# Scores of the second token group by three fp32r products, and its probabilities normalised behind the product with the values

## The chip, the cores and the metric

The kernel runs on one core of one Trainium2 chip. The metric is the time of one execution on the device in microseconds (us), given as the median of the runs shown. TensorE (PE in the profile) multiplies matrices, VectorE (DVE) and ScalarE (ACT) work element by element, GpSimd (POOL) hardly takes part, and SyncE (SP) issues most DMAs. Each engine works through its own instructions in the order in which the program gives them.

## The reference, cut to what matters

```python
# attention: batch 2, 12 heads, 448 tokens, head size 64, causal
scores = (q @ k.T) / sqrt(64);  scores[j > i] = -1e9
p = exp(scores - max(scores));  p = p / (sum(p) + 1e-9)
x = (p @ v) reshaped to 896 tokens x 768
# first layer: 768 -> 2048 -> 768
h = x @ w_in;  g = h if h >= 1, 0 if h <= -1, (h + 1)**2 / 4 between
y = g @ w_out
# second layer: 768 -> 1536 -> 768
out = (silu(y @ w_gate) * (y @ w_val)) @ w_out2
```

All inputs and the output are fp32. q and k are scaled up by about 22, so that the scores are large and need nearly full fp32 precision.

## The kernel before

The time has two parts. In the first, the attention is worked out and, from its middle on, the first products of the first layer are slipped in between. In the second, only the large products of the two layers run.

The attention works by units. A unit is one batch and one pair of heads for one of two token groups: group 0 is the first 224 tokens of each sequence, group 1 the last 224. There are 12 units of group 0, of one step each, and then 12 units of group 1, of two steps each: step kind 2 has 112 tokens against 336 keys, kind 3 has 112 tokens against all 448. The two heads of a pair lie in partitions 0 to 63 and 64 to 127 of one tile `qk_t`. A step goes through these functions:

- `scores`: PE multiplies q and k of each head in plain fp32 into the PSUM tile `s`, and adds the causal mask as one more product (`mask_b` times an identity, bf16).
- `greatest`: DVE takes the row maxima (`tensor_reduce`, L427) and scales them (`mx`, L429).
- `exps`: ACT takes the exponentials into `p` and their row sums into `sm` (L441).
- `normalize`: DVE turns the sums into reciprocals (L452, L453) and multiplies `p` by them (L465).
- `turn` and `turned`: PE transposes `p` into the PSUM tile `t`, and ACT copies it to `pt` (L485).
- `values`, once a unit: PE multiplies `pt` and the values into the PSUM tile `o`.
- `x_hi`, `x_lo`: ACT rounds `o` to fp32r (`xh`, L518) and DVE takes the rest (`xl`, L522).

The layers multiply split operands: each fp32 matrix is the sum of two fp32r parts, hi and lo, and `mm3` issues three fp32r products, hi hi, hi lo and lo hi. The weights come in a narrowing form and are made into such parts in four operations (L102, L105, L108 and the pair L213 on ACT and L214 on DVE, called a tick each here). `Weights.tick` issues the next of these, and `TICKS` and `LATER` say how many at each step of the two groups.

The loop of the attention runs over steps k. At each k it goes through the list `ORDER[kind]`, and each word in it issues one function, for step k+1, k, k-1 or k-2. `fill` issues in group 0 a few products of zeros (`zeros`, L532), and from step 14 on a third of the 18 products of one 128-column block of the first layer for group 0 (`h_products`, tile `mm`, one PSUM bank). When a block is complete, ACT and DVE work out its activation (`h_relu` L341, `h_max` L346 and L347, `g_hi` L352, `g_lo` L356), and only L347 frees the bank for the next block. `follow` keeps an issued group of products together on PE; the rest of the order on each engine is set by a list scheduler at build time from the order of issue and its priorities, which is why the order is shown below beside the diff.

Of the kernel before, what the change touches and what calls it, by code (L numbers as in the profile page):

```python
# [8 lines left out]
F32 = mybir.dt.float32  # L9
F32R = mybir.dt.float32r  # L10
# [20 lines left out]
HOLD = (12, 6, 4, 2)  # L31
AHEAD = 3
LASTB = 2
WBUFS = 4
# [4 lines left out]
LOW_V = 999  # L39
NORM_P = 0  # L40
TURN0 = "A"
TURN1 = "A"
NORM0 = "V"
NORM1 = "V"
SEVEN = (1, 2, 3, 4, 5, 6, 7, 8, 9, 10)
# [8 lines left out]
S_LOW = "V"  # L54
PINNED = 2

ORDER = {
    0: "copy scores max fill values x_hi weights norm x_lo turn exp relu square g_hi g_lo".split(),
    2: "copy scores fill max relu values exp norm x_hi x_lo turn square g_hi g_lo weights".split(),
    3: "copy scores fill max relu values exp norm x_hi x_lo turn square g_hi g_lo weights".split(),  # L60
}
TICKS = (1, 0, 1)
LATER = (1, 0, 3)


@with_exitstack
def fused_kernel(ctx: ExitStack, tc: tile.TileContext, qk, v, w_in, w_out, w_gv, w_o2, out):
# [3 lines left out]
    edge = ctx.enter_context(tc.tile_pool(name="edge", bufs=1, side="right"))  # L71
    half_b = edge.tile([128, 56], F32, name="half_b")[:, :1]
    half_x = const.tile([128, 32], F32, name="half_x")[:, :1]
    xy = ctx.enter_context(tc.tile_pool(name="xy", bufs=2))
# [246 lines left out]
    def bank():  # L321
        pool = banks.pop(0)
        banks.append(pool)
        return pool.tile([128, 512], F32, tag="mm", name="mm")

    def h_products(g, f, free=((True, True), (True, True))):

        xh, xl = xT[g]
        wh, wl = W.get(f)
        ps = bank()  # L330
        for c in range(KC):
            sl = slice(c * 128, (c + 1) * 128)
            mm3(ps[:, :N], wh[:, sl], wl[:, sl], xh[:, c], xl[:, c], c == 0, c == KC - 1, free[c % 2])
            if c % 2 and c < KC - 1:
                yield
        yield ps

    def h_relu(f, ps):

        r = ev.tile([128, N], F32, tag="r", name="r")  # L340
        nc.scalar.activation(out=r, in_=ps[:, :N], func=AF.Relu, bias=half_b, scale=0.5)  # L341
        return f, ps, r

    def h_max(f, ps, r):
        q = ev.tile([128, N], F32, tag="t", name="q")
        nc.vector.scalar_tensor_tensor(out=q, in0=r, scalar=1.0, in1=r, op0=ALU.min, op1=ALU.mult)  # L346
        nc.vector.tensor_tensor(out=q, in0=ps[:, :N], in1=q, op=ALU.max)  # L347
        return 0, f, q, gt0
# [22 lines left out]
    with ExitStack() as ph:  # L371
# [7 lines left out]
        mask_b = lp.tile([128, C], BF16, name="mask_b")  # L379
        ld, st, pts = {}, {}, {}  # L380

        def load(u):
            if u >= len(units):
                return
            g, n = units[u]
            src = n[0] * NP + n[1]
            qk_t = lp.tile([128, 672], F32, tag="qk", name="qk_t", bufs=AHEAD + 1)
            v_t = lp.tile([C, 4, 128], F32, tag="v", name="v_t", bufs=AHEAD + 4)
# [6 lines left out]
            ld[u] = qk_t, v_t  # L395

        def scores(k):
# [6 lines left out]
            for i, (off, w, q0) in enumerate(reversed(SEGS[j])):  # L404
                for h in range(2):
                    hd = slice(h * D, (h + 1) * D)
                    follow(
                        nc.tensor.matmul, i == h == 0,
                        out=s[:C, h, off:off + w], lhsT=qk_t[hd, q0:q0 + C], rhs=qk_t[hd, k0:k0 + w],
                        start=(i == 0), stop=False, skip_group_check=True,  # L410
                    )
            for off, w, _ in SEGS[j]:
                for h in range(2):
                    follow(
                        nc.tensor.matmul, False,
                        out=s[:C, h, off + w - C:off + w], lhsT=ident_b[:C, :], rhs=mask_b[:C, :],
                        start=False, stop=True, skip_group_check=True,
                    )
            st[k] = {"s": s}

        def greatest(k):

            _, j = steps[k]
            s, segs = st[k]["s"], SEGS[j]
            mx = s[:C, 0, 504:508].rearrange("p (i h) -> p i h", h=2)
            for i, (off, w, _) in enumerate(segs):
                nc.vector.tensor_reduce(out=mx[:, i], in_=s[:C, :, off:off + w], axis=AX.X, op=ALU.max)  # L427
            m = pp.tile([C, 2, 2], F32, tag="mx", name="mx")
            nc.vector.tensor_scalar(  # L429
                out=m[:, :len(segs)], in0=mx[:, :len(segs)], scalar1=-0.125, scalar2=None, op0=ALU.mult)  # L430
            st[k]["mx"] = m

        def exps(k):

            _, j = steps[k]
            s, mx = st[k]["s"], st[k]["mx"]
            sm = pp.tile([C, 2, 2], F32, tag="sm", name="sm")
            p = pp.tile([C, 2, S], F32, tag="p", name="p")
            for i, (off, w, _) in enumerate(SEGS[j]):
                for h in range(2):  # L440
                    nc.scalar.activation(  # L441
                        out=p[:, h, off:off + w], in_=s[:C, h, off:off + w], func=AF.Exp,
                        bias=mx[:, i, h:h + 1], scale=0.125, accum_out=sm[:, i, h:h + 1],
                    )
            st[k].update(p=p, sm=sm)

        def normalize(k):
            _, j = steps[k]
            p, segs = st[k]["p"], SEGS[j]
            sm = st[k].pop("sm")  # L450
            m = sm[:, :len(segs)]
            nc.vector.tensor_scalar(out=m, in0=m, scalar1=1e-9, scalar2=None, op0=ALU.add)  # L452
            nc.vector.reciprocal(out=m, in_=m)  # L453
            for i, (off, w, _) in enumerate(segs):
                if j == 0 and NORM_P:
                    nc.gpsimd.tensor_tensor(
                        out=p[:, :, off:off + w], in0=p[:, :, off:off + w],
                        in1=sm[:, i].unsqueeze(2).to_broadcast([C, 2, w]), op=ALU.mult,
                    )
                else:  # L460
                    norms = NORM0 if j == 0 else NORM1
                    for h in range(2):
                        ph, r = p[:, h, off:off + w], sm[:, i, h:h + 1]
                        if norms[(2 * k + h) % len(norms)] == "V":
                            nc.vector.tensor_scalar(out=ph, in0=ph, scalar1=r, scalar2=None, op0=ALU.mult)  # L465
                        else:
                            nc.scalar.mul(out=ph, in_=ph, mul=r)

# [19 lines left out]
        def values(k):  # L488
# [25 lines left out]
            g, (b, hp) = units[u]  # L514
            return [o[:, :GT]] + [t[:, hp, b * GT:(b + 1) * GT] for t in xT[g]]

        def x_hi(o, xh, xl):
            nc.scalar.copy(out=xh, in_=o)  # L518
            return o, xh, xl

        def x_lo(o, xh, xl):
            nc.vector.tensor_tensor(out=xl, in0=o, in1=xh.bitcast(F32), op=ALU.subtract)  # L522

# [6 lines left out]
        def zeros(n):  # L530
# [4 lines left out]
        make_identity(nc, ident)  # L535
        nc.vector.memset(mask_b, 0.0)
        nc.vector.memset(half_b, 0.5)

        nc.scalar.activation(out=half_x, in_=half_b, func=AF.Exp)
        nc.gpsimd.affine_select(  # L540
            out=mask_b[:C, :], in_=mask_b[:C, :], compare_op=ALU.is_ge, fill=MASK,
            base=0, pattern=[[-1, C]], channel_multiplier=1,
        )
# [18 lines left out]
        first1 = next(k for k, (u, j) in enumerate(steps) if j == 2)  # L562
        fresh_o, half_o, half, whole, split_h = [], [], [], [], []
        for k in range(-1, last + 2):
# [3 lines left out]
            for op in ORDER[kind]:  # L568
# [4 lines left out]
                elif op == "max" and lead:  # L573
                    greatest(k + 1)
                elif op == "exp" and lead:
                    exps(k + 1)
# [5 lines left out]
                elif op == "values" and pv:  # L582
                    assert not fresh_o and not half_o and "t" not in st[k - 2]
                    fresh_o.append(values(k - 2))
                elif op == "x_hi" and fresh_o:
                    half_o.append(x_hi(*fresh_o.pop()))
                elif op == "x_lo" and half_o:
# [20 lines left out]
        while done < EARLY or fresh or half or whole or split_h:  # L608
# [8 lines left out]
            if done < EARLY:  # L617
                filler()
                W.tick()
        assert not fresh_o and not half_o  # L620

# [288 lines left out]
```

## Time and profile before

| what | us |
|---|---|
| runs | 585.08, 597.69, 585.05 |
| median | 585.08 |
| profiled execution, its own time | 585.47 |
| its span, first to last instruction | 583.7 |
| attention with the first products in it | about 0 to 146 |
| products of the layers alone | about 146 to 583.7 |

[...] PE is busy 575.5 us, DVE 489.8 us and ACT 271.1 us. Busy times overlap a little: an instruction's time begins before the one ahead of it has ended, so that the distance from start to start is the better measure of what one costs.

### The profile page before, as it was taken

The page shows a single profiled execution, that of the slowest core. Times are in us where ns is not written, and L with a number is a line of the kernel's source. Part 1 is how long each engine was busy: PE and PEld are TensorE (multiplying, and loading weights), DVE is VectorE, ACT ScalarE, POOL GpSimd, SP SyncE. Part 2 cuts the span into 40 slices and gives each one's busy share as a digit, 9 for nine tenths or more (in the row PEclk, how much of TensorE's full clock was granted, in tenths as well). Part 3 has the DMA queues.
Part 4 walks back from the last instruction along what each step waited for, and adds up shares of the span by engine and source line. Part 5 has one row for each costly group of instructions (what it writes and reads, how often), then busy time and mean ns, then how long its engine had stood idle before and what let it go on. Part 6 is the DMA issues. An engine that isn't in the chain of part 4 may idle for free.

```text
span 583.7 us, 8503 instructions
## 1 busy us (share of the span) xinstructions
PE 575.5 (99%) x3167; PEld 498.8 (85%) x3172; DVE 489.8 (84%) x899; ACT 271.1 (46%) x544; POOL 0.9 (0%) x7
## 2 busy tenths in 40 slices
PE   9999999998999999999999999999999999999997
PEld 5766766667999999999999999999999999999996
DVE  2999999973896988787778899999898398999990
ACT  3887777664533444111211165554454244346441
POOL 0000000000000000000000000000000000000000
PEclk9999999999999999999999999999999999999999
DMA  8566554300131233787788711363532133730011
GB/s 259 173 182 210 174 188 144 136 2 2 55 118 45 90 109 120 230 269 207 238 292 244 271 68 56 108 190 108 176 107 98 55 115 109 277 127 16 17 62 65
DMA packets 26009, 80.38 MB, mean 138 GB/s; under 512 B 2928, under 2 KB 10672, under 8 KB 25968
## 3 DMA queue, kind: packets, MB, share of 16 engines
q1 hardware_dynamic: 21792, 73.54, 39.1%
q10 hardware_dynamic: 4176, 6.29, 2.9%
q8 instruction: 25, 0.41, 0.3%
q14 instruction: 16, 0.13, 0.1%
HBM read 70.78 MB, written 9.04 MB: 137 GB/s over the span
## 4 chain that ended last, share of the span: by engine, by line
PE 83%; DVE 13%; ACT 2%; DMA 1%; issue 0%; ACTq 0%
PE mm L84 35%; PE mm L719 27%; PE mm L849 13%; DVE s L427 3%; DVE p L465 2%; PE mm L86 2%; PE s L84 1%; DVE wt L108 1%; PE mm L532 1%; DVE wt L105 1%; ACT p L441 1%; DVE wl L214 1%; DMA wraw<-w_in 1%; PE s L86 1%; PE t L86 1%; DVE wt L102 1%
## 5 line engine op out<-in xcount | busy, mean ns | idle before, releaser
L213 ACT CAST wh<-wt 128x768 fp32r<-128x768 f32 (+1 forms) x43 | 34.7, 807 | 94.2 <-PE mm L84 46.9
L84 PE MATMUL mm<-gl,wh 128*128 128x448 f32 x192 | 70.1, 365 | 0.0
L84 PE MATMUL mm<-gh,wh 128*128 128x448 f32 x192 | 70.1, 365 | 0.0
L84 PE MATMUL mm<-gh,wl 128*128 128x448 f32 x192 | 70.1, 365 | 0.0
L84 PE MATMUL mm<-xh,wh 128*128 128x448 f32 x165 | 62.5, 379 | 2.3 <-DVE q L347 2.3
L441 ACT ACTIVATE p<-s,mx 112x112 f32<-112x112 f32 (+3 forms) x96 | 46.3, 496 | 20.6 <-DVE mx L429 15.1
L84 PE MATMUL mm<-xh,wl 128*128 128x448 f32 x138 | 50.4, 365 | 0.0
L84 PE MATMUL mm<-xl,wh 128*128 128x448 f32 x138 | 50.4, 365 | 0.0
L214 DVE TENSOR_TENSOR wl<-wt,wh 128x768 fp32r<-128x768 f32 (+1 forms) x43 | 39.4, 916 | 10.0 <-ACT wh L213 9.6
L105 DVE SCALAR_TENSOR_TENSOR wt<-wraw,wt 128x768 int32<-128x768 int32 (+1 forms) x51 | 47.1, 923 | 0.8
L108 DVE SCALAR_TENSOR_TENSOR wt<-wraw,wt 128x768 int32<-128x768 int32 (+1 forms) x51 | 47.0, 922 | 0.5
L849 PE MATMUL mm<-ul,oh 128*128 128x448 f32 x126 | 46.0, 365 | 0.0
L849 PE MATMUL mm<-uh,oh 128*128 128x448 f32 x126 | 46.0, 365 | 0.0
L849 PE MATMUL mm<-uh,ol 128*128 128x448 f32 x126 | 46.0, 365 | 0.0
L427 DVE TENSOR_REDUCE s<-s 112x2 f32<-112x224 f32 (+3 forms) x48 | 35.4, 744 | 7.5 <-PE s L86 7.4
L719 PE MATMUL mm<-yh,wh 128*128 128x448 f32 x108 | 39.4, 365 | 0.0
L719 PE MATMUL mm<-yh,wl 128*128 128x448 f32 x108 | 39.4, 365 | 0.0
L719 PE MATMUL mm<-yl,wh 128*128 128x448 f32 x108 | 39.4, 365 | 0.0
L84 PEld LDWEIGHTS mm<-gl,wh 128*128 128x128 f32 x192 | 36.1, 188 | 2.9
L84 PEld LDWEIGHTS mm<-gh,wl 128*128 128x128 f32 x192 | 36.1, 188 | 2.9
L84 PEld LDWEIGHTS mm<-gh,wh 128*128 128x128 f32 x192 | 36.1, 188 | 2.8
L84 PEld LDWEIGHTS mm<-xh,wh 128*128 128x128 f32 x165 | 31.0, 188 | 5.6 <-DVE q L347 3.4
(140 smaller groups left out, 1366.4 us busy)
## 6 DMA issues: line engine op xcount, KB each, us to landing
wraw<-w_in SPq DMA_DIRECT2D x16, 768.0 KB, 4.5
wraw<-w_gv SPq DMA_DIRECT2D x14, 768.0 KB, 4.4
wraw<-w_out SPq DMA_DIRECT2D x12, 768.0 KB, 4.9
araw<-w_gv SPq DMA_DIRECT2D x20, 384.0 KB, 4.6
wraw<-w_o SPq DMA_DIRECT2D x9, 768.0 KB, 4.3
n<-at ACTq DMA_DIRECT2D x26, 192.0 KB, 4.5
qk_t<-qk SPq DMA_DIRECT2D x12, 336.0 KB, 3.3
wraw<-n SPq DMA_DIRECT2D x5, 768.0 KB, 4.3
```

Of the source, the lines that this page charges most:

```text
L84: return product(*args, **kw)
L86: return tc.keep_in_program_order(product(*args, **kw))
L102: yield nc.vector.tensor_scalar(out=t, in0=w[:, :, 1], scalar1=3, scalar2=0x3FFFFFF8, op0=ALU.logical_shift_left, op1=ALU.bitwise_and,)
L105: yield nc.vector.scalar_tensor_tensor(out=t, in0=w[:, :, 1], scalar=-0x40000000, in1=t, op0=ALU.bitwise_and, op1=ALU.bitwise_or,)
L108: yield nc.vector.scalar_tensor_tensor(out=t, in0=w[:, :, 0], scalar=29, in1=t, op0=ALU.logical_shift_right, op1=ALU.bitwise_or,)
L213: nc.scalar.copy(out=wh[:, :n], in_=t)
L214: (nc.vector if i < LOW_V else nc.gpsimd).tensor_tensor(out=wl[:, :n], in0=t, in1=wh[:, :n].bitcast(F32), op=ALU.subtract,)
L427: nc.vector.tensor_reduce(out=mx[:, i], in_=s[:C, :, off:off + w], axis=AX.X, op=ALU.max)
L441: nc.scalar.activation(out=p[:, h, off:off + w], in_=s[:C, h, off:off + w], func=AF.Exp, bias=mx[:, i, h:h + 1], scale=0.125, accum_out=sm ...
L465: nc.vector.tensor_scalar(out=ph, in0=ph, scalar1=r, scalar2=None, op0=ALU.mult)
L719: nc.tensor.matmul(out=ps[:, :N], lhsT=w[a][:, sl], rhs=rows[c][b], start=(first and c == i == 0), stop=(last and c == i == 2), skip_group ...
L849: nc.tensor.matmul(out=ps, lhsT=w[a][:, sl], rhs=rows[c][b], start=(not more and c == e == 0), stop=(c == 5 and e == 2), skip_group_check= ...
```

## The change

For group 1 the parts hi and lo of `qk_t` are made once a unit (`apart_qk`: ACT copies to `qh`, DVE subtracts to `ql`), and the scores are three fp32r products of them for each head, in place of one fp32 product. In steps of kind 2 the mask is no longer a product: DVE's `tensor_tensor_reduce` adds a mask tile, scales by -0.125, writes `s` back and takes the minimum, for each head, which is the bias that the exponential wants; the reduction and L429 fall away there. Steps of kind 3 keep the mask product and the reduction. `normalize` no longer multiplies `p` in group 1. The sums of a unit's two steps lie in one tile, whose reciprocals are taken once a unit; four small fp32 products with a broadcast operand bring them into the layout of `o`, in the same bank; ACT copies them out (`rb`), and DVE multiplies `o` by them (`x_norm`). The parts `xh` and `xl` are then made from `rb`.

The lists in `ORDER` are written anew, with the words `x` and `apart`; `TICKS` gives one tick in three steps in group 0 in place of two, `LATER` four in three steps as before but spread differently; `PINNED` goes from 2 to 9. Ahead of two blocks of the first layer in group 1 stands a product of 1 x 8 (`strip`). The branches under `HM` don't run.

```diff
-PINNED = 2
+PINNED = 9
+STRIPS = (1, 2)
+TTR = (2,)
+HM = 0
...
-    2: "copy scores fill max relu values exp norm x_hi x_lo turn square g_hi g_lo weights".split(),
+    2: "copy turn scores fill max values relu x norm x_hi square x_lo exp g_hi g_lo apart weights".split(),
...
-TICKS = (1, 0, 1)
-LATER = (1, 0, 3)
+TICKS = (0, 0, 1)
+LATER = (1, 1, 2)
...
+        def apart_qk(u):
...
+            hi = lp.tile([128, 672], F32R, tag="qh", name="qh", bufs=QB)
+            lo = lp.tile([128, 672], F32R, tag="ql", name="ql", bufs=QB)
+            split(raw, hi, lo)
...
+            if j:
+                (off, w, q0), = SEGS[j]
+                hi, lo = halves[u]
+                for i, (a, b) in enumerate(((hi, hi), (hi, lo), (lo, hi))):
+                    for h in range(2):
+                        hd = slice(h * D, (h + 1) * D)
+                        follow(
+                            nc.tensor.matmul, i == h == 0,
+                            out=s[:C, h, off:off + w], lhsT=a[hd, q0:q0 + C], rhs=b[hd, k0:k0 + w],
...
-            for off, w, _ in SEGS[j]:
+            for off, w, _ in () if j in TTR else SEGS[j]:
...
+            if j in TTR:
+                off, w, _ = segs[0]
+                for h in range(2):
+                    part = s[:C, h, off:off + w]
+                    nc.vector.tensor_tensor_reduce(
+                        out=part, in0=part, in1=mask[:, S - w:], scale=-0.125, scalar=3.0e38,
+                        op0=ALU.add, op1=ALU.min, accum_out=m[:, 0, h:h + 1],
+                    )
...
+            if j == 2:
+                return
+            sm = sms[u]
+            nc.vector.tensor_scalar(out=sm, in0=sm, scalar1=1e-9, scalar2=None, op0=ALU.add)
+            nc.vector.reciprocal(out=sm, in_=sm)
+            if j == 0:
...
+            for i in range(2 if j else 0):
+                for h in range(2):
+                    follow(
+                        nc.tensor.matmul, False, out=o[h * D:(h + 1) * D, 256 + i * C:256 + (i + 1) * C],
+                        lhsT=sm[:, i, h:h + 1].to_broadcast([C, D]), rhs=ident[:C, :C],
...
+            if j:
+                r = pp.tile([128, GT], F32, tag="rb", name="rb", bufs=2)
+                nc.scalar.copy(out=r, in_=o[:, 256:256 + GT])
...
+        def x_norm(o, r, xh, xl):
+            if r is None:
+                return o, xh, xl
+            nc.vector.tensor_tensor(out=r, in0=o, in1=r, op=ALU.mult)
+            return r, xh, xl
```

On PE, in the middle of group 1, the scores of a step of kind 2 and what follows them stood like this before (`s` scores, `mm` products slipped in, `o` values, `t` transposes; L84 and L86 are lines of the helpers):

```order
L84 MATMUL s<-qk_t 112x336
L86 MATMUL s<-qk_t 112x336
L86 LDWEIGHTS ident_b
L86 MATMUL s<-mask_b,ident_b 112x112
...
L84 MATMUL mm<-xh,wh 128x448
...
L84 MATMUL o<-pt,v_t 64x224
L86 MATMUL o<-pt,v_t 64x224 x5
L86 MATMUL o<-pt,v_t 64x112 x2
L84 MATMUL t<-ident,p 112x112
```

And so they stand in the change, where L89 and L91 are the same lines of the helpers:

```order
L89 MATMUL s<-qh 112x336
L91 MATMUL s<-qh 112x336
L91 MATMUL s<-ql,qh 112x336 x2
L91 MATMUL s<-qh,ql 112x336 x2
L89 MATMUL o<-pt,v_t 64x224
L91 MATMUL o<-pt,v_t 64x224 x5
L91 MATMUL o<-pt,v_t 64x112 x2
L91 MATMUL o<-ident,sm 64x112 x4
L89 MATMUL mm<-xh,wh 128x448
```

Six score products stand for two, the mask products are gone, four products of the sums follow the values, and here, where a new block begins, the products slipped in come behind the values and no longer ahead of them.

On DVE, in the middle of group 1, one stretch of a unit before (`s` reduction, `p` normalising, `q` and `gl` activation of a block, `wt` a tick):

```order
L465 TENSOR_SCALAR p<-p,sm 112x336 x2
L346 SCALAR_TENSOR_TENSOR q<-r 128x448
L427 TENSOR_REDUCE s<-s 112x2
L347 TENSOR_TENSOR q<-mm,q 128x448
L429 TENSOR_SCALAR mx<-s 112x2
L452 TENSOR_SCALAR sm<-sm 112x2
L522 TENSOR_TENSOR xl<-o,xh 128x224
L453 RECIPROCAL sm<-sm 112x2
L105 SCALAR_TENSOR_TENSOR wt<-wraw,wt 128x768
```

The same place in the change, where the two rows named ISA are the masked reduction and the row that writes out its result:

```order
L577 TENSOR_TENSOR rb<-o,rb 128x224
L374 TENSOR_TENSOR gl_3_1414<-q,gh_3_1413 128x448
L478 TENSOR_REDUCE s<-s 112x2
L585 TENSOR_TENSOR xl<-rb,xh 128x224
L479 TENSOR_SCALAR mx<-s 112x2
L101 TENSOR_TENSOR ql<-qk_t,qh 128x672
L471 ISA s,mx<-s,mask 112x336
L471 ISA mx 112x1
L504 TENSOR_SCALAR sm<-sm 112x4
```

The normalising of `p` is gone, and `rb`, `ql` and the masked reduction have come in.

On PE near the end of the attention, where the seventh block (`mm_1627` before) ends and the eighth (`mm_1748`) begins:

```order
L86 MATMUL mm_1627<-xl_75,wh_1435 128x448
L86 MATMUL mm_1627<-xh_74,wl_1436 128x448
L84 MATMUL t_1731<-ident_102,p_1638 112x112
L86 MATMUL t_1731<-ident_102,p_1638 112x112 x3
...
L84 MATMUL mm_1748<-xh_74,wh_1566 128x448
```

In the change these blocks are `mm_1739` and `mm_1865`:

```order
L91 MATMUL mm_1739<-xh_75,wl_1619 128x448
L89 MATMUL t_1858<-ident_103,p_1806 112x112
L91 MATMUL t_1858<-ident_103,p_1806 112x112 x2
...
L89 MATMUL o_1872<-pt_1813,v_t_1420 64x224
L91 MATMUL o_1872<-pt_1813,v_t_1420 64x224 x5
...
L91 MATMUL o_1872<-ident_103,sm_1705 64x112 x4
L89 MATMUL t_1899<-ident_103,p_1847 112x112
L91 MATMUL t_1899<-ident_103,p_1847 112x112 x3
...
L89 MATMUL mm_1865<-xh_75,wh_1759 128x448
```

Between the two blocks there was one group of transposes, and now there are two and the values of a unit.

## Rows read from the trace of the kernel before

**Rows 1.** The page's first part: busy us, share of span, instructions.

```profile
PE 575.5 (99%) x3167; PEld 498.8 (85%) x3172; DVE 489.8 (84%) x899; ACT 271.1 (46%) x544; POOL 0.9 (0%) x7
```

**Rows 2.** Windows by stage: length, busy us of each engine, clock, DMA share.

```profile
15.00:45.00 30.00, 29.55 (x272) 20.40 (x272) 29.64 (x109) 26.83 (x104) 0.00 (x0) 1.00 0.63 186
45.00:80.00 35.00, 34.78 (x250) 23.48 (x246) 35.00 (x91) 25.86 (x64) 0.00 (x0) 1.00 0.57 186
...
110.00:146.00 36.00, 33.84 (x234) 25.13 (x231) 22.26 (x58) 19.54 (x48) 0.00 (x0) 1.00 0.09 34
146.00:347.00 201.00, 201.00 (x993) 186.25 (x993) 165.47 (x276) 61.02 (x98) 0.00 (x0) 1.00 0.53 171
```

**Rows 3.** The chain that ended last: start, length, what.

```profile
146.17 200.64 PE mm L84 x990
```

**Rows 4.** Timeline of PE over one unit of group 1: start, length, instruction.

```profile
113.30 0.63 PE L84 MATMUL s<-qk_t 64*112 64x448 f32 x1
113.31 0.63 PE L86 MATMUL s<-qk_t 64*112 64x448 f32 x1
113.77 0.54 PE L84 MATMUL s<-qk_t 64*112 64x448 f32 x1
...
114.24 0.31 PE L86 MATMUL s<-mask_b,ident_b 112*112 112x112 bf16 x2
114.37 0.45 PE L84 MATMUL mm<-xh,wh 128*128 128x448 f32 x1
114.65 0.36 PE L86 MATMUL mm<-xl,wh 128*128 128x448 f32 x1
...
115.67 0.26 PE L84 MATMUL t<-ident,p 112*112 112x112 f32 x1
...
116.53 0.53 PE L84 MATMUL s<-qk_t 64*112 64x336 f32 x1
...
117.28 0.31 PE L86 MATMUL s<-mask_b,ident_b 112*112 112x112 bf16 x2
117.41 0.45 PE L84 MATMUL mm<-xh,wh 128*128 128x448 f32 x1
...
118.84 0.40 PE L84 MATMUL o<-pt,v_t 112*64 112x224 f32 x1
...
120.32 0.31 PE L84 MATMUL t<-ident,p 112*112 112x112 f32 x1
...
121.04 0.63 PE L84 MATMUL s<-qk_t 64*112 64x448 f32 x1
```

**Rows 5.** Windows of nine middle units, the last of them and their sum.

```profile
121.04:128.72 7.68, 7.68 (x55) 5.32 (x55) 4.91 (x15) 4.36 (x12) 0.00 (x0) 1.00 0.00 0
sum 71.49, PE 70.31 PEld 48.25 DVE 66.88 ACT 49.49 POOL 0.00; mean PE 7.81 PEld 5.36 DVE 7.43 ACT 5.50 POOL 0.00
```

**Rows 6.** The chain between 90 and 112 us, all on DVE.

```profile
93.59 0.61 DVE p L465 x2
...
94.67 0.77 DVE s L427
...
97.03 0.73 DVE p L465 x2
97.76 0.53 DVE q L347
98.29 0.30 DVE xl L522
...
101.13 0.85 DVE wl L214
```

**Rows 7.** Groups on ACT from 57 to 129 us: count, busy us, mean ns.

```profile
L213 ACT CAST wh<-wt 128x768 fp32r<-128x768 f32 x6 | 5.0, 836 | 5.9 <-DVE wt L108 5.9
...
L518 ACT CAST xh<-o 128x224 fp32r<-128x224 f32 x10 | 3.5, 346 | 0.7 <-PE o L86 0.6
```

**Rows 8.** Timeline of PE near the end of the attention, with its wait.

```profile
131.57 0.45 PE L86 MATMUL t<-ident,p 112*112 112x112 f32 x3
133.30 0.47 PE L84 MATMUL mm<-xh,wh 128*128 128x448 f32 x1 [1.27 <-DVE q L347]
```

More of the change, by code (lines that the diff above doesn't have):

```diff
@@ L32 @@
 AHEAD = 3
+QB = 2
+VB = AHEAD + 4
+PB = 3
+QKB = AHEAD + 1
 LASTB = 2
@@ L39 @@
 LOW_V = 999
-NORM_P = 0
 TURN0 = "A"
 TURN1 = "A"
-NORM0 = "V"
-NORM1 = "V"
 SEVEN = (1, 2, 3, 4, 5, 6, 7, 8, 9, 10)
@@ L54 @@
 S_LOW = "V"
-PINNED = 2
+PINNED = 9
+STRIPS = (1, 2)
+TTR = (2,)
+HM = 0
 ORDER = {
-    0: "copy scores max fill values x_hi weights norm x_lo turn exp relu square g_hi g_lo".split(),
-    2: "copy scores fill max relu values exp norm x_hi x_lo turn square g_hi g_lo weights".split(),
-    3: "copy scores fill max relu values exp norm x_hi x_lo turn square g_hi g_lo weights".split(),
-}
-TICKS = (1, 0, 1)
-LATER = (1, 0, 3)
+    0: "copy scores fill values x x_hi apart weights x_lo max turn exp g_hi relu norm square g_lo".split(),
+    2: "copy turn scores fill max values relu x norm x_hi square x_lo exp g_hi g_lo apart weights".split(),
+    3: "norm copy turn scores fill max values x relu exp apart x_hi square g_hi g_lo weights x_lo".split(),
+}
+TICKS = (0, 0, 1)
+LATER = (1, 1, 2)
 @with_exitstack
@@ L324, in bank, with strip @@
         return pool.tile([128, 512], F32, tag="mm", name="mm")
+    def strip(ps, w, x):
+        nc.tensor.matmul(
+            out=ps[:1, 448:456], lhsT=w[:, :1], rhs=x[:, :8], start=True, stop=True, skip_group_check=True)
     def h_products(g, f, free=((True, True), (True, True))):
@@ L330, in h_products @@
         ps = bank()
+        if g and f in STRIPS:
+            strip(ps, wh, xh[:, 0])
         for c in range(KC):
@@ L395, in load @@
             ld[u] = qk_t, v_t
+        halves = {}
+        def apart_qk(u):
+            if not (0 <= u < len(units) and units[u][0]):
+                return
+            raw = ld[u][0]
+            hi = lp.tile([128, 672], F32R, tag="qh", name="qh", bufs=QB)
+            lo = lp.tile([128, 672], F32R, tag="ql", name="ql", bufs=QB)
+            split(raw, hi, lo)
+            halves[u] = hi, lo
         def scores(k):
@@ L402, in scores @@
             k0 = GT if j == 0 else 0
-            for i, (off, w, q0) in enumerate(reversed(SEGS[j])):
+            if j:
[7 more added lines that the diff above has]
+                            out=s[:C, h, off:off + w], lhsT=a[hd, q0:q0 + C], rhs=b[hd, k0:k0 + w],
+                            start=(i == 0), stop=i == 2 and j in TTR, skip_group_check=True,
+                        )
+            for i, (off, w, q0) in enumerate(() if j else reversed(SEGS[j])):
                 for h in range(2):
@@ L514, in values, with x_hi, x_lo @@
             g, (b, hp) = units[u]
[L515 to L522, printed above, removed]
+            sm = sms.pop(u)
+            for i in range(2 if j else 0):
[3 more added lines that the diff above has]
+                        lhsT=sm[:, i, h:h + 1].to_broadcast([C, D]), rhs=ident[:C, :C],
+                        start=True, stop=True, skip_group_check=True,
+                    )
+            if j:
+                r = pp.tile([128, GT], F32, tag="rb", name="rb", bufs=2)
+                nc.scalar.copy(out=r, in_=o[:, 256:256 + GT])
+            else:
+                r = None
+            return [o[:, :GT], r] + [t[:, hp, b * GT:(b + 1) * GT] for t in xT[g]]
+        def x_norm(o, r, xh, xl):
[3 more added lines that the diff above has]
+            return r, xh, xl
+        def x_hi(x, xh, xl):
+            nc.scalar.copy(out=xh, in_=x)
+            return x, xh, xl
+        def x_lo(x, xh, xl):
+            nc.vector.tensor_tensor(out=xl, in0=x, in1=xh.bitcast(F32), op=ALU.subtract)
         for u in range(AHEAD):
@@ L541, in fused_kernel @@
             out=mask_b[:C, :], in_=mask_b[:C, :], compare_op=ALU.is_ge, fill=MASK,
+            base=0, pattern=[[-1, C]], channel_multiplier=1,
+        )
+        nc.gpsimd.affine_select(
+            out=mask[:, S - C:], in_=mask[:, S - C:], compare_op=ALU.is_ge, fill=MASK,
             base=0, pattern=[[-1, C]], channel_multiplier=1,
@@ L562, in fused_kernel @@
         first1 = next(k for k, (u, j) in enumerate(steps) if j == 2)
-        fresh_o, half_o, half, whole, split_h = [], [], [], [], []
+        fresh_o, whole_o, half_o, half, whole, split_h = [], [], [], [], [], []
         for k in range(-1, last + 2):
@@ L574, in fused_kernel @@
                     greatest(k + 1)
+                elif op == "apart" and lead and steps[k + 1][1] != 2:
+                    apart_qk(steps[k + 1][0] + 1)
                 elif op == "exp" and lead:
@@ L619, in fused_kernel @@
                 W.tick()
-        assert not fresh_o and not half_o
+        assert not fresh_o and not whole_o and not half_o
     gt1 = gctx.enter_context(tc.tile_pool(name="gt1", bufs=1))
```

79 lines of the change are left out of this document (41 added, 38 removed).

## The prediction

> **What bounds the kernel now.** I read the page's busy times first: PE 99% of the span, DVE 84%, ACT 46% [rows 1]. A share over the whole span says little, so next come the windows by stage. From 146 us on PE is busy without a gap, and the chain that ended last runs there through nothing but products, 200.64 us for 990 of them, 0.203 us each [rows 2, 3]. The change touches none of these, so the 437.5 us from there to the end stay. Everything is decided between 0 and 146 us.
>
> There DVE looks like the bound: 29.64 of 30 us in group 0, 35.00 of 35 us from 45 to 80, and the chain runs through DVE's instructions one after the other [rows 2, 6]. But PE reads 34.78 of 35 in the same window. To see which of the two sets the pace I followed PE's timeline through one unit of group 1, start to start [rows 4]: scores of the 448 step 0.94 (113.30 to 114.24), their mask 0.13, six products slipped in 1.30, eight transposes 0.86, scores of the 336 step 0.75, mask 0.13, six products 1.43, values 1.48, six transposes 0.72. That is 7.74, and nothing in it is a gap except about 0.1 in the 1.43. The shortest unit lasts 7.68 us, and the nine middle units together 71.49 [rows 5], so PE stood still for 71.49 - 9 x 7.68 = 2.4 us in all of them. PE is the bound of group 1, with DVE close behind (66.88 busy in 71.49), until DVE runs out of ticks at about 111 us and idles (22.26 of the last 36) [rows 2, 5]. A lighter DVE is worth only the gaps of PE; a lighter PE counts twelvefold.
>
> **PE, part by part.** A plain fp32 product runs as two instructions: 0.47 from 113.30 to 113.77, and as long again to the mask. The two heads start 0.01 us apart, so they run side by side, in different rows of the array [rows 4]. An fp32r product of 448 columns costs 1.30 / 6 = 0.217 with its share of the edges. 0.94 is 4.3 times that, so I read a fp32 product as four such passes, 0.87, and 0.07 of edge. For 336 columns the same gives 0.163 a pass and 0.10 of edge in the 0.75. Three passes and the same edge: 3 x 0.217 + 0.07 = 0.72, and 3 x 0.163 + 0.10 = 0.59. With the mask of the 336 step gone (0.13) a unit saves 0.22 + 0.16 + 0.13 = 0.51. If no edge were left, 0.68; if each product paid a whole edge, 0.51 - 2 x 0.07 - 2 x 0.10 = 0.17.
>
> The four products that spread the sums are new. The values, fp32 too and in the same layout, take 1.48 for 784 columns of each head [rows 4]; 224 more columns are 0.42. At the price of transposes, 0.12 for one of 112 columns, eight instructions not side by side would be 0.96. I take 0.42, since they have the shape of the values and stand right behind them. Per unit PE then changes by -0.51 + 0.42 = -0.09, twelve units -1.1 us. The bounds are -0.68 + 0.42 = -0.26 (-3.1 us) and -0.17 + 0.96 = +0.79 (+9.5 us). So the three products save about what the sums cost.
>
> [...]
>
> **DVE and ACT.** Per unit DVE loses the normalising of `p`, 0.61 + 0.73, one reduction, 0.77, and three small rows of about 0.07 [rows 6]: 2.32. It gains two masked reductions of 336 columns; the nearest row reads PSUM and SBUF as they do, 0.53 for 448 columns, and `xl` 0.30 for 224, hence 0.42 each, and 0.07 to write each result, 0.97. The split adds 0.85 x 672 / 768 = 0.74, and `x_norm` a copy of `xl`, 0.30. Net -2.32 + 2.01 = -0.31 a unit, -3.7 us in all. Four ticks move out of group 0 (4 x about 0.85) into the end of group 1, where DVE idled. ACT gains a copy of 672 columns (0.836 x 672 / 768 = 0.73) and one of 224 (0.35) [rows 7], +1.08 on a mean of 5.50 in a unit of 7.68 [rows 5]: covered while nothing waits for ACT at once. Queued behind the copy to `qh` are the exponentials and the copy to `pt`. For the latter PE's order helps: between the eight transposes and the values that need their copy there now stand the 448 scores, six products, six transposes and the 336 scores, some 3.5 us, where 0.88 and 1.3 stood before.
>
> **Gaps of PE.** Of the 2.4 us in the middle units I take 2.0 back, as DVE no longer runs full. Near the end PE waits 1.27 us for L347 to free the bank [rows 8]; by the new order 0.72 + 1.48 + 0.42 + 0.86 of other work lies there, so 1.2 goes. In group 0 PE has 0.45 us without work in 30 [rows 2], and its zero products stay as many; fewer ticks give back at most that, 0.4. Against it I set 1.0 for new waits on ACT, which gets 20% more work (bounds 0 and 3; a tenth of a unit's 1.08 each time), and 0.2 for the two 1 x 8 products.
>
> **Sum.** 585.47 is the profiled execution's own time, 583.7 of it span. -1.1 - 2.0 - 1.2 - 0.4 + 1.0 + 0.2 = -3.5, so 582.0; it lies 0.4 above the median of the runs, which makes **581.6 us**. About 2%, 11.7 us, is what a measurement of this kernel can tell from no change; the forecast lies within it.
>
> **Rivals.**
> - *Every product pays its weight load.* Scores save 0.17 a unit, not 0.51: 12 x 0.34 = +4.1, 585.7 us. For it: 0.47 and 0.47 can be read so. [...] Chance 0.15. [...]
> - *The masked reduction runs at half rate.* 24 x 0.42 = +10 us on DVE, +6.4 with its savings. That is 6.4 / 12 = 0.53 a unit; DVE then sets the pace (7.43 + 0.53 = 7.96 against 7.68, 12 x 0.28 = 3.4), and nothing else is won: 585.1 + 3.4 = 588.5 us. For it: no row shows this instruction. Against: its two inputs are read at full rate in `q`. [...] Chance 0.07.
> - *The heads don't run side by side in the new products.* Scores cost 6 x 0.217 + 0.07 = 1.37 and 6 x 0.163 + 0.10 = 1.08, a unit +0.43 + 0.20, and the sums 0.84: +1.47, against -0.09 in the forecast 1.56 x 12 = 18.7 us more, 600 us. This is the slower side. It decides from about 1.2 us a unit on. For it: an fp32r product in half the rows stands nowhere in the trace. Against: the fp32 ones with the same rows do pair. Chance 0.05.
> - *PE gets all of it.* No edges (-3.1), all gaps (2.4 + 1.3 + 0.4), no waits on ACT: 585.1 - 7.2 + 0.2 = 578.1, and 575.6 if the sums' products hide half of their 0.42. Chance 0.15.
>
> **How the numbers follow.** The forecast's own cluster, 578.5 to 585, has 0.58. The range, 575.5 to 588.6, takes in the fast rival, the paid loads and the half rate, and leaves out the unpaired heads and what I don't foresee. Faster by over 2% (below 573.4) needs more than all gaps and all edges, 0.05; slower by over 2% (above 596.8) is the unpaired heads, 0.05; within 2% 0.90.
>
> **What will show it.** Scores on PE in the changed profile: 0.72 and 0.59 from their start to the next group, or 0.80 and more each if loads are paid, or 1.1 to 1.4 if unpaired. The sums' products: 0.42 between values and next group. Masked reductions on DVE 0.42 apart, or 0.8. A unit about 7.6 us, and the products alone starting at about 142.6 rather than 146.2. The prediction is wrong if PE waits for `pt` or `p` in each unit (ACT), or if the stage after 146 us changes.

## The result, and the profile after

The changed kernel takes 590.5 us (591.06, 590.13, 590.80, 590.20). Against the kernel before the ratio is 1.0094, interval 1.0069 to 1.0118: under 1% slower, and outside the forecast range on the slower side. The kernel before has executions of two kinds, near 585 and near 594 us (the fourth, run beside the changed kernel, took 594.54); ratios here are against the lower kind.

The profiled execution took 591.06 us, 589.3 of it span, with a mean granted clock of 1.000, as in the kernel before (1.000). The page's busy times hardly differ from [rows 1]:

```profile
PE 582.5 (99%) x3294; PEld 505.8 (86%) x3294; DVE 489.4 (83%) x877; ACT 280.6 (48%) x568; POOL 1.2 (0%) x8
```

The chain that ended last tells where the time is: start, length, what. This is the changed kernel from the end of the attention on; its row for 990 products in [rows 3] is here the first three together, split by the two 1x8 products:

```profile
144.51 3.71 PE mm L89 x18
148.23 3.76 PE mm L89 x18
151.99 197.10 PE mm L89 x954
349.09 159.16 PE mm L792 x774
508.25 77.66 PE mm L922 x378
```

And the two rows of the kernel before that follow the one in [rows 3]:

```profile
346.81 156.87 PE mm L719 x774
503.68 76.62 PE mm L849 x378
```

The attention ends 1.66 us earlier (144.51 for 146.17; the prediction had 142.6). The same 2142 products then take 3.71 + 3.76 + 197.10 + 159.16 + 77.66 = 441.39 us, against 200.64 + 156.87 + 76.62 = 434.13: 206.1 ns each in place of 202.7, +7.26 us. -1.66 + 7.26 = 5.6, which is the difference of the spans. In neither trace does PE wait there, and the clock is the same (1.00): the products follow each other at another spacing. From start to start over eighteen products or more, the trace of before shows 202.7 ns throughout. That of the changed kernel shows 206.7 up to 148 us, 203 behind the first 1x8 product, 206.7 again from 159.4 us to 367 us, and from there 206.7 in blocks of some operands and about 204.4 in those of others.

The timeline of PE in one unit of the changed kernel (start, length, instruction; [rows 4] are those of before):

```profile
112.34 0.45 PE L89 MATMUL s<-qh 64*112 64x448 f32 x1
112.34 0.46 PE L91 MATMUL s<-qh 64*112 64x448 f32 x1
112.63 0.37 PE L91 MATMUL s<-ql,qh 64*112 64x448 f32 x2
112.83 0.37 PE L91 MATMUL s<-qh,ql 64*112 64x448 f32 x2
113.14 0.31 PE L91 MATMUL s<-mask_b,ident_b 112*112 112x112 bf16 x2
...
115.24 0.41 PE L89 MATMUL s<-qh 64*112 64x336 f32 x1
...
115.89 0.47 PE L89 MATMUL mm<-xh,wh 128*128 128x448 f32 x1
...
117.31 0.40 PE L89 MATMUL o<-pt,v_t 112*64 112x224 f32 x1
...
119.17 0.31 PE L89 MATMUL t<-ident,p 112*112 112x112 f32 x1
...
120.08 0.45 PE L89 MATMUL s<-qh 64*112 64x448 f32 x1
```

Scores take 0.80 (112.34 to 113.14) and 0.65, the values with the sums 1.86 (117.31 to 119.17). The window of this unit, with the columns of [rows 5], has no gap on PE:

```profile
112.34:120.08 7.74, 7.74 (x65) 5.93 (x65) 7.61 (x17) 5.89 (x14) 0.00 (x0) 1.00 0.19 50
```

PE's waits between 128 and 150 us, in the changed kernel and then in the kernel before (who waits for whom: us, times, longest), where [rows 8] show the 1.27:

```profile
PE t L89 <- ACT p L493: 0.7, 1, 0.7
PE mm L89 <- DVE q L365: 0.4, 1, 0.4
```

```profile
PE mm L84 <- DVE q L347: 1.8, 2, 1.3
```

Some of DVE's and ACT's new groups, 57 to 129 us (count, busy us, mean ns of one, which overlaps its neighbours):

```profile
L471 DVE CUSTOM_DVE_ANT_0 s<-s,mask 112x336 f32<-112x336 f32 x18 | 9.2, 509 | 1.4 <-PE s L91 1.3
...
L471 DVE DVE_READ_ACCUMULATOR2_ANT mx<- 112x1 f32 x18 | 2.5, 141 | 0.0
```

```profile
L100 ACT CAST qh<-qk_t 128x672 fp32r<-128x672 f32 x8 | 6.1, 766 | 0.0
```

DVE's timeline in the same unit gives their distances from start to start, the measure of [rows 6]:

```profile
111.69 0.38 DVE L577 TENSOR_TENSOR rb<-o,rb 128x224 f32<-128x224 f32 x1
111.99 0.95 DVE L219 TENSOR_TENSOR wl<-wt,wh 128x768 fp32r<-128x768 f32 x1
...
115.62 0.84 DVE L101 TENSOR_TENSOR ql<-qk_t,qh 128x672 fp32r<-128x672 f32 x1
116.39 0.15 DVE L479 TENSOR_SCALAR mx<-s 112x2 f32<-112x2 f32 x1
...
118.03 0.51 DVE L471 CUSTOM_DVE_ANT_0 s<-s,mask 112x336 f32<-112x336 f32 x1
118.45 0.14 DVE L471 DVE_READ_ACCUMULATOR2_ANT mx<- 112x1 f32 x1
118.45 0.17 DVE L505 RECIPROCAL sm<-sm 112x4 f32<-112x4 f32 x1
```

Eight units take the stretch from 66 to 128 us. Its row (columns of [rows 2]), in the kernel before and then in the changed one:

```profile
66.00:128.00 62.00, 61.00 (x426) 42.01 (x422) 58.11 (x144) 41.83 (x99) 0.00 (x0) 1.00 0.40 129
66.00:128.00 62.00, 62.00 (x518) 47.89 (x518) 53.02 (x124) 50.40 (x124) 0.00 (x0) 1.00 0.34 109
```

So the question is what changed the spacing of products that the change doesn't touch.

### The profile page after: what moved, and what is told of

Same layout as the page of the kernel before. It is cut to its first block, busy times and chain, and to the rows that moved or that the text cites. A ratio compares the mean times of both kernels' runs of the same rounds, so it can differ in the third digit from the quotient of the medians.

```text
span 589.3 us, 8754 instructions
## 1 busy us (share of the span) xinstructions
PE 582.5 (99%) x3294; PEld 505.8 (86%) x3294; DVE 489.4 (83%) x877; ACT 280.6 (48%) x568; POOL 1.2 (0%) x8
## 4 chain that ended last, share of the span: by engine, by line
PE 91%; DVE 4%; ACT 3%; issue 0%; ACTq 0%
PE mm L89 36%; PE mm L792 27%; PE mm L922 13%; PE mm L91 4%; PE o L91 2%; ACT p L493 2%; PE s L91 2%; PE t L91 2%; PE s L89 2%; PE o L89 1%; PE mm L595 1%; PE t L89 1%; DVE s L478 1%; DVE wt L110 1%; ACT pt L529 1%; DVE wt L113 0%
## 5 line engine op out<-in xcount | busy, mean ns | idle before, releaser
L89 PE MATMUL mm<-gh,wh 128*128 128x448 f32 x192 | 70.7, 368 | 0.0
L89 PE MATMUL mm<-gl,wh 128*128 128x448 f32 x192 | 70.7, 368 | 0.0
L89 PE MATMUL mm<-gh,wl 128*128 128x448 f32 x192 | 70.7, 368 | 0.0
L89 PE MATMUL mm<-xh,wh 128*128 128x448 f32 x165 | 62.9, 381 | 0.5 <-DVE q L365 0.4
L89 PE MATMUL mm<-xl,wh 128*128 128x448 f32 x138 | 50.8, 368 | 0.0
L89 PE MATMUL mm<-xh,wl 128*128 128x448 f32 x138 | 50.8, 368 | 0.0
L89 PEld LDWEIGHTS mm<-gh,wh 128*128 128x128 f32 x192 | 36.0, 188 | 3.7
L89 PEld LDWEIGHTS mm<-gl,wh 128*128 128x128 f32 x192 | 36.0, 188 | 3.7
L89 PEld LDWEIGHTS mm<-gh,wl 128*128 128x128 f32 x192 | 36.0, 188 | 3.5
L89 PEld LDWEIGHTS mm<-xh,wh 128*128 128x128 f32 x165 | 31.0, 188 | 5.8 <-issue 1.3
L792 PE MATMUL mm<-th,sh 128*128 128x448 f32 x90 | 33.1, 368 | 0.0
```

The source lines that it names most:

```text
L89: return product(*args, **kw)
L792: nc.tensor.matmul(out=ps[:, :N], lhsT=w[a][:, sl], rhs=rows[c][b], start=(first and c == i == 0), stop=(last and c == i == 2), skip_group ...
```

## The experiments

The diff holds one more thing, which the prediction passed over and the lines printed ahead of it leave out: a tile `one_b` of 8 numbers, 32 bytes a partition, at the very top of the right side, beside `half_b` (its only readers stand under `HM`, which is 0), and a memset that fills it. Pools of the right side are laid out below it. In the built programs all operands of the 2142 products stand at multiples of 256 bytes in the kernel before. In the changed one those in right-side pools stand at a remainder of 224, 32 bytes off a multiple of 64: five weight blocks that are kept (`stay`, read by blocks four to eight of group 1, numbered from 0), the row sums (`tp`) and one of the two pools of the last stage (`ua`). Block four begins at 159.2 us, where the quick spacing ends:

```profile
159.02 0.36 PE L89 MATMUL mm<-xh,wl 128*128 128x448 f32 x1
159.22 0.36 PE L89 MATMUL mm<-xh,wh 128*128 128x448 f32 x1
159.43 0.37 PE L89 MATMUL mm<-xl,wh 128*128 128x448 f32 x1
159.63 0.37 PE L89 MATMUL mm<-xh,wl 128*128 128x448 f32 x1
```

There is no wait, and nothing on PE's queue but the next block. In the last stage, where blocks of 54 products read `ua` and the other pool (`ub`, in place) by turns, it is the blocks of `ua` that take 204.5 ns, and those of `ub` 206.6. Theory 1 is the placement: a product that reads an off tile throws the stream out of a quick rhythm (202.7 ns a product), and the slow one (206.7) keeps itself. Theory 2: the way in which the stream comes out of the attention decides. Theory 3: the chip was slow for both kernels.

**Without the tile** (`after_no_tile`).

```diff
-    one_b = edge.tile([128, 8], F32, name="one_b")[:, :1]
...
-        nc.vector.memset(one_b, 1.0)
```

> The changed kernel without its tile of 32 bytes a partition on the right side (one_b, which nothing reads, and the memset that fills it). Theory 1, placement: that tile pushes every later tile of the right side to an address that is 32 bytes off a multiple of 64, and a product that reads such a tile throws TensorE's stream out of its quick rhythm (202.7 ns a product) into slower ones (206.7 or 204.4 ns), out of which it does not come back by itself. Then all blocks from the first 1x8 product on stay at 202.7 ns, the 2142 products from 144.5 us on take 434.3 us instead of 441.0, and the profiled run takes 591.06 - 6.7 = 584.4 us. Theory 2, the start of the stream: the rhythm is set by how the stream comes out of the attention, addresses do not matter; then this edit changes nothing, 590 to 591 us. Theory 3, this chip or session is slow for both kernels: 590 to 591 us, and the kernel before near 594 us beside it.

583.35 us median, ratio 0.9969 (0.9956 to 0.9982). Its chain:

```profile
144.07 3.65 PE mm L88 x18
147.73 3.75 PE mm L88 x18
151.49 193.45 PE mm L88 x954
344.94 156.86 PE mm L790 x774
501.80 76.62 PE mm L920 x378
```

3.65 + 3.75 + 193.45 + 156.86 + 76.62 = 434.33, as theory 1 said; theory 3 is gone. One row speaks for a part of theory 2: the first block runs at 3.65 / 18 = 203 ns already before the first 1x8 product.

**The kernel before with the tile** (`before_plus_tile`).

```diff
     half_b = edge.tile([128, 56], F32, name="half_b")[:, :1]
+    one_b = edge.tile([128, 8], F32, name="one_b")[:, :1]
...
+        nc.vector.memset(one_b, 1.0)
```

> The kernel before with only the unread tile of 32 bytes a partition and its memset added. Theory 1, placement: the stream of products alone, 434.1 us at 202.7 ns in the kernel before, falls out of the quick rhythm at the fifth block of the second group at the latest (its weights are right-side tiles) and takes 439 to 443 us; 591 to 594 us in every execution. Theory 2, the start of the stream: nothing changes, 585 us (or 594 to 598 where the kernel before shows that). Theory 3: whatever the kernel before shows beside it.

592.22 us, ratio 1.0125 (1.0110 to 1.0140).

```profile
145.76 204.31 PE mm L85 x990
350.07 159.16 PE mm L721 x774
509.23 77.66 PE mm L851 x378
```

204.31 + 159.16 + 77.66 = 441.13, the changed kernel's sum within 0.3. The spacing is 202.7 ns from 146 us on and 206.7 from 160.4, where block four begins (145.76 and 72 products). So 32 unread bytes make the whole loss, without any other part of the change.

**A tile of 256 and of 64 bytes** (`after_tile_256`, `after_tile_64`).

```diff
-    one_b = edge.tile([128, 8], F32, name="one_b")[:, :1]
+    one_b = edge.tile([128, 64], F32, name="one_b")[:, :1]
```

For 64 bytes the tile is `[128, 16]`.

> The changed kernel with the same unread tile made 256 bytes a partition instead of 32. Theory 1, placement: all right-side tiles are back on multiples of 256, so the quick rhythm of 202.7 ns holds from 148.1 us to the end and the profiled run takes about 584.4 us, although the tile and its memset are still there. Theory 2 (start of the stream) and theory 3 (chip): as the changed kernel, 590 to 591 us with 206.7 ns a product from 159.4 us on.

> The changed kernel with the unread tile made 64 bytes a partition (16 numbers): right-side tiles stand on multiples of 64 that are none of 256. If 64 is enough, the stream stays at 202.7 ns behind the 1x8 product at least to the first block that reads sums, 583 to 588 us; if it takes 256, it goes as the changed kernel, 206.7 ns from 159 us on and 590 to 591 us.

Once each: 587.58 us for 256 bytes, 584.27 for 64. With 256 the quick rhythm outlasts the kept blocks, as theory 1 says, but ends at 367 us in a block of seven products, so 584.4 was missed by 3.2. There the trace has one weight load some 20 ns late (366.33, behind 366.11), just after the end of ScalarE's copy to `two`, which frees its bank (365.75 + 0.53 = 366.28); from then on it is 206.7 ns to the end, with every tile in place. That this small wait did it fits, but is only argued. With 64 bytes nothing falls at the kept blocks: their 90 products take 200.0 ns each (158.14 to 176.14 us), less than in either rhythm, and 202.7 follow (the chain's row for 954 products reads 193.21 us, 193.45 in `after_no_tile`). From 366 us on, where the row sums are read, the products of the off pools (`tp`, `ua`) take about 202 ns and those with all tiles in place about 206.5, up to the end (a block of `ub`, 512.73 to 523.89 us: 206.6). So in this run the products that read tiles 64 bytes off a multiple of 256 are the quick ones (200.0 and about 202 ns), but here too the slow rhythm has come in, and it keeps itself wherever the tiles are in place (206.5). Why it came in where moving operands were off by 64, and not where weights were, stays open.

**One more 1x8 product at each block of seven** (`tile_256_rekick`), in the kernel with the 256-byte tile.

```diff
+        strip(banks3[0], gate[0], chunks(0, 0)[0][0])
         add(a, gate, 0, chunks(0, 0), True, True)
```

> The kernel with the 256-byte tile, whose stream fell from 202.7 to 206.7 ns at 367 us behind a wait of some 20 ns for ScalarE and stayed there, with one more 1x8 product at the start of each of the ten blocks of seven products (10 x 0.1 us). Theory 1 with a rhythm that keeps itself: at the next block the stream is back at 202.7 ns, so it loses at most one block (63 x 4 ns = 0.25 us) at each slip, and the run takes 587.6 - 4.0 + 1.0 + 0 to 1 = 584.6 to 585.6 us. If a wait that comes back in each block is what sets the pace there, the stream is slow again behind each, 587.5 to 588.6 us.

584.31 us, once. The stream was quick in all of it (its last row reads 76.62 us for 378, 202.7 ns), so there was no fall to mend: the time fits, but the run doesn't tell the two readings apart.

**Only the 1x8 products, in the kernel before** (`before_plus_strips`).

```diff
...
+        if g and f in (1, 2):
+            strip(ps, wh, xh[:, 0])
```

> The kernel before with only the two products of 1x8 added, ahead of the second and third block of the second group. Theory 1 with theory 2's start: the kernel before has the quick rhythm in some executions (585.05, 585.08 us) and a slow one in others (594.54, 597.69 us), as the stream happens to begin; the 1x8 products put it into the quick one whatever the start, so all executions come out at 585.1 to 585.6 us, none near 594. If the two products do not set the rhythm: both kinds of time again, 585 and 594 to 598 us. If they only cost: 585.3 us (2 x 0.1 us more than 585.05) beside 594 and more.

All twelve executions lie between 584.58 and 586.16; of the twenty of the kernel before beside them nine took 593.3 us or more. In its profile the stream came out of the attention slow, and the first 1x8 product set it right:

```profile
145.60 3.72 PE mm L84 x18
149.32 3.76 PE mm L84 x18
153.09 193.44 PE mm L84 x954
```

3.72 / 18 = 206.7 ns; then 193.44 / 954 = 202.8. The two kinds of the kernel before lie some 8.6 us apart, 2142 x 4.0 ns; no profile of the higher kind was taken, so that they are the same two rhythms is inferred. In all, 41 of 81 executions of the kernel before took 592 us or more; of the changed kernel without the tile (`after_no_tile` and the next run) all sixteen lie between 582.87 and 584.07.

**Without tile and 1x8 products** (`no_tile_no_strips`).

```diff
-STRIPS = (1, 2)
+STRIPS = ()
```

> The changed kernel without the unread tile and without its two 1x8 products. Theory 1, placement with a rhythm that keeps itself: the attention leaves the stream in the slow rhythm (206 ns a product up to 148 us in the changed kernel) and nothing puts it into the quick one, so the 2142 products take 442.5 instead of 434.3 us and the run takes 583.35 + 8.2 = 591.6 us, although every tile is on a multiple of 256. Theory 2, placement alone: with all tiles in place the stream finds the quick rhythm by itself, as it does in the profile of the kernel before, 583.2 us.

583.25 us, all ten between 582.87 and 583.89: my 591.6 was wrong. The stream is quick from its first product (144.47 us, 200.64 for 990, 202.7 ns). With tiles in place the changed attention handed it over quick here, and also in the profiles of `after_no_tile` and `tp_off_32` (3.65 us for the first 18 in both, 203 ns), but slow in that of `after_tile_256` (3.72, 206.7 ns). In this run leaving out the 1x8 products costs nothing. Theory 2's point stands as half of the truth: in these runs the handover sets the rhythm, and off tiles end it. What in the attention sets it stays open.

**Off tiles in one pool only** (`stay_off_32`, `tp_off_32`): no tile on top, 32 bytes under the kept blocks, or under the row sums.

```diff
     stay = ExitStack()
+    off = stay.enter_context(tc.tile_pool(name="off", bufs=1, side="right")).tile([128, 8], F32, name="off")
+    nc.vector.memset(off, 0.0)
```

> The changed kernel without the unread tile on top of the right side, but with 32 bytes a partition under the one pool of the five kept weight blocks, so only their tiles stand 32 bytes off a multiple of 64; they are the stationary operand of 90 of the 2142 products alone (blocks four to eight of the second group, 159 to 178 us) and of filling products in the attention. All other operands are on multiples of 256. Theory 1, a rhythm that keeps itself: TensorE falls to 206.7 ns a product at 159 us and stays there to the end, (2142 - 72) x 4 ns = 8.3 us, 591.6 us. If only the products that read an off tile are slow: 90 x 4 ns = 0.4 us, 583.7 us.

> The changed kernel without the unread tile, with 32 bytes a partition under the one pool of the row sums, the moving operand of 360 products in the ten blocks of seven products; all else on multiples of 256. Theory 1, a rhythm that keeps itself: quick to about 366 us, then 206.7 and 204.4 ns in turns as in the changed kernel to the end of those blocks at 476 us and 206.7 ns from there to the end: 630 x 2.9 ns + 486 x 4 ns = 3.8 us, 587.1 us. If only the products that read an off tile are slow: 360 x 1.7 to 4 ns, 584 to 584.8 us.

591.57 us (forecast 591.6) and, once, 586.93 (587.1). In the first, 90 products of 2142 read an off tile, and they end at 178 us; yet all that follow are slow:

```profile
151.08 197.10 PE mm L88 x954
348.18 159.96 PE mm L792 x774
508.14 78.13 PE mm L922 x378
```

78.13 / 378 = 206.7 ns, 330 us behind the last off tile. In the second the stream is quick to 366 us, and the last stage, with nothing off, takes 78.13 us as well.

**The same with one interruption** (`stay_off_rekick`).

```diff
-STRIPS = (1, 2)
+STRIPS = (1, 2, 9)
```

> The kernel with 32 bytes a partition under the pool of the kept weight blocks (591.57 us; off tiles read only up to 178 us, yet 206.7 ns a product to the end), with one more 1x8 product ahead of the tenth block of the second group, the second block that reads no off tile any more. Theory 1, a rhythm that keeps itself: from there on 202.7 ns a product, slow only in blocks four to eight of the second group and the first block behind them, 108 x 4 ns + 0.1 = 0.5 us more than 583.35, so 583.9 us. If something else that the 32 bytes moved keeps the stream slow (other addresses, other timing on VectorE or ScalarE), the 1x8 product changes nothing for good: 591.6 us.

584.02 us. The second of these rows ends at the added product:

```profile
147.92 3.76 PE mm L88 x18
151.69 29.70 PE mm L88 x144
181.39 164.27 PE mm L88 x810
345.66 156.86 PE mm L792 x774
502.52 76.63 PE mm L922 x378
```

164.27 / 810 = 202.8 ns. The addresses are those of `stay_off_32`; one product of 8 columns, about 0.1 us, gives back 7.5 us. So other addresses or other timing are not what keeps it slow. In these two runs the slow rhythm is a state of the stream that keeps itself.

**The attention's parts, each undone, without the tile** (`no_tile_fp32_scores`, `no_tile_mask_product`, `no_tile_norm_ahead`).

```diff
-                for i, (a, b) in enumerate(((hi, hi), (hi, lo), (lo, hi))):
+                for i, (a, b) in enumerate(((qk_t, qk_t),)):
...
-TTR = (2,)
+TTR = ()
...
-            for i in range(2 if j else 0):
+            for i in range(0):
```

The first also leaves out the split of q and k, and the third also takes back the multiplication of `p` and leaves out `rb`.

> The changed kernel without the unread tile, with the scores of the second group by one fp32 product as before, not by three fp32r products; q and k are not split (the ScalarE copy of 0.77 us and the VectorE subtraction of 0.85 us a unit go). Everything else of the change stays, the normalising behind the values and the masked reduction. If TensorE sets the pace of the second group's units: its scores go back from 0.79 to 0.94 us and from 0.64 to 0.75 us, 0.25 us a unit, 3.0 us over twelve units, so the products alone begin at 147 us and the run takes 586.4 us. If VectorE or ScalarE set it: no change or a gain, 582.5 to 583.4 us.

> The changed kernel without the unread tile, with the mask of the 336-column step added by a TensorE product and a plain reduction as before, not by the masked reduction. TensorE gets 0.13 us a unit back, VectorE loses 2 x (0.51 + 0.14) - 0.87 - 0.15 = 0.28 us a unit. If TensorE sets the pace: 583.3 + 1.6 = 584.9 us. If VectorE sets it: down to 580 us. If neither: 583.3 us.

> The changed kernel without the unread tile, with the probabilities of the second group normalised ahead of the transposes on VectorE as before (four products with the reciprocals a unit); the sums' products, ScalarE's copy of their result and VectorE's multiplication by it go. Split scores and masked reduction stay. If TensorE alone sets the pace of the second group: 0.38 us a unit less, 583.3 - 12 x 0.38 = 578.7 us. If VectorE takes over: it was busy for 53.1 us of the 62 of eight units, and gets 2 x 0.455 + 2 x 0.396 + 0.34 - 0.39 = 1.65 us a unit more, 66.3 us, so the units grow by 0.5 us each to 589 us.

587.39, 585.28 and 586.73 us, against 583.35. The stream alone begins at 148.03, 146.18 and 147.68 us, against 144.07, and runs at 202.7 ns in all three. The first two follow TensorE's price (3.0 and 1.6 us forecast, 4.0 and 1.9 measured; with fp32 scores PE also waits 2.0 us for L364, 0.4 without). In the second VectorE is as busy as with the masked reduction (53.01 and 53.09 of the 62 us from 66 to 128): the 0.28 that it was to lose were summed from busy times, which overlap, so the run weighs TensorE's product alone. In the third PE has 12 x 0.38 = 4.6 us less to do and still ends 3.6 us later. VectorE is busy 59.35 of the 62 us, and PE's longest waits are

```profile
PE o L88 <- ACT pt L531: 3.9, 5, 1.0
```

behind transposes that now start only when `p` is normalised. That is the direction that I gave for VectorE as the bound, at 60% of its price (3.4 of 5.7 us). The price was summed from busy times too; from start to start the 1.65 a unit are about 0.61 + 0.73 + 0.14 - 0.30 = 1.18. That VectorE, and not the longer way from `p` to `pt`, holds PE there is argued, not shown.

## Why the prediction was wrong, point by point

**The step that failed** is "The change touches none of these, so the 437.5 us from there to the end stay." They became 589.3 - 144.51 = 444.8, +7.3, all of it in the spacing of products that no line of the change names. I read the 0.203 us as a price of a product [rows 3]. It is one of two rhythms, and the tile that ends it was in the change. I looked at what the change computes, and not at where its allocations push the rest. With that one tile gone the changed kernel takes 583.35 us: within the forecast's own cluster, 1.75 above its 581.6. It lies there although of the 3.5 us that were to come off the attention only 1.66 did, and 2.10 without the tile. With 32 bytes under the kept weight blocks alone the loss is 591.57 - 583.35 = 8.2 us (`stay_off_32` against `after_no_tile`).

**TensorE's part** was right in mechanism, too large in size. Scores save 0.94 - 0.80 + 0.75 - 0.65 + 0.13 = 0.37 a unit, not 0.51: the middle of the three products takes 0.20 (112.63 to 112.83), the first and the last 0.29 and 0.31, so there is more edge than 0.07. The rival in which every product pays a weight load would have saved 0.17. It wants an edge on the middle product too, 0.217 + 0.07 in the larger step. The trace doesn't agree: the middle product's 0.20 is what a product costs in the stream alone, and its loads start 0.09 us behind the first products of both heads (112.34, 0.45 long), in the same partitions, and 0.20 ahead of the product itself:

```profile
112.43 0.18 PEld L91 LDWEIGHTS s<-ql,qh 64*112 64x112 f32 x2
```

The 0.80 of the larger step stands where my sign for paid loads stood ("0.80 and more"), the 0.65 of the smaller below it; the extra lies in the first and the last product, and what makes it is open. The sums cost 0.38 (0.42 forecast). Net -0.37 + 0.38 = 0.01 a unit: nothing is won, where -1.1 us were forecast for the twelve.

**Gaps.** The units have none left, as forecast. The wait of 1.27 [rows 8] went, but 0.7 for ScalarE's `p` and 0.4 for L365 came in its place. PE's listed waits from 15 to 150 us fall from 3.2 to 1.9: -1.3, against -2.0 - 1.2 - 0.4 + 1.0 = -2.6 forecast. With 0.1 for twelve units of TensorE's part that is 1.2 of the 1.66 by which the attention got shorter; the rest would lie in gaps too short for that list. In the middle units the term of 2.0 came nearly whole: eight of them, from scores to scores, take 61.5 us (66.26 to 127.81) in place of 63.3 (65.38 to 128.72).

**VectorE and ScalarE** came as forecast. From start to start a masked reduction costs 0.42 (118.03 to 118.45), as forecast, although its busy time reads 0.51, and reading out its result costs nothing where the next instruction starts with it (118.45 twice), not 0.07. The split takes 0.77 (0.74 forecast) and `x_norm` 0.30. That is 0.84 + 0.77 + 0.30 = 1.91 a unit added, not 2.01, against 2.32 taken away. Over eight units VectorE is busy 53.02 us in place of 58.11; three ticks fewer in that stretch (21 for 24) are about half of it. So VectorE is lighter, and with PE full (7.74 of 7.74) that is worth only the gaps, as the prediction said. ScalarE's copy to `qh` (0.77, forecast 0.73) is hidden in the unit shown. None of the rivals on the engines happened: the two heads start together (112.34 twice), with scores of 0.80 and 0.65 and not 1.1 to 1.4, and the masked reduction takes 0.42, not 0.8.

## What to carry to other kernels

Every allocation of a change belongs to it, a tile that nothing reads as well: ask which pools it moves, and by how much. Where a long stream of equal products decides the time, compare its spacing from start to start before and after, before any theory of engines; 4 ns on 2142 products outweighed all that was tuned in the attention. Price an instruction by the distance from its start to the next start: sums of busy times made VectorE seem dearer than it was. And an operation that moves an engine's work elsewhere is judged with what takes its place: three products and the sums cancel on TensorE, yet with the rest of the change in place going back on any one part costs 1.9 to 4.0 us.

## What the runs showed of the hardware that was not expected

- A stream of fp32r products of 128x448 by 128x128 without a wait had two steady spacings at the same granted clock (1.00): 206.7 ns (the changed kernel from 159.4 us on), and 202.7 ns (the kernel before), the mean of a pattern that comes back every five products (202, 203, 199, 207, 202). A stream stayed in the slow one for over 400 us (`stay_off_32`, from 159 us to the end).
- Operands 32 bytes off a multiple of 64 ended the quick one within a block, without a wait: weights (`stay_off_32`, at 159 us) and moving rows (`tp_off_32`, at 366 us) alike. In the changed kernel the products that went on reading them took 206.7 ns for weights and about 204.4 for moving rows, and those with all tiles in place behind them 206.7.
- Weights 64 bytes off a multiple of 256 gave 200.0 ns over 90 products, less than with all tiles in place (`after_tile_64`, one run).
- A product of 1x8, about 0.1 us, put a slow stream into the quick one, from 206.7 to about 203 ns a product (`before_plus_strips` at 149.2 us, `stay_off_rekick` at 181 us, the changed kernel at 148.1 us).
